# Nystrom attention and squared-ReLU MLP on one core: attention relaid by landmark segment, transposes moved from the DMA queue to TensorE and VectorE, instruction order written out as a table

## The chip, the core and the metric

One core of a Trainium2 chip. The time is device microseconds of one execution; 278.01 us is the median of three runs before the change (278.54, 278.01, 274.76).

## What is computed

For 8 batches of 8 heads, with q, k, v of 576 tokens by 64 (32 segments of 18 tokens each; a landmark is the mean of one segment):

```
q_lm, k_lm = segment means of q and k              # 32 x 64 a head
A  = softmax(q @ k_lm^T / 8)                       # 576 x 32
Bm = softmax(q_lm @ k_lm^T / 8)                    # 32 x 32
C  = softmax(q_lm @ k^T / 8)                       # 32 x 576
Z  = Bm^T / (norm1 * norminf);  6 times: Z = 2 Z - Z @ Bm @ Z
x  = A @ Z @ C @ v                                 # heads side by side: 4608 x 512
out = relu(x @ w_in)**2 @ w_out                    # 512 -> 2048 -> 512
```

## The kernel before

Batches follow each other. `attention(b)` makes, for one batch, AT (A transposed, heads on the partitions) and G (Z C v w_in, the product with `w_in` taken in early). `mlp_in(b)` forms h = G^T AT in 16 blocks of 128 hidden rows (L938, four matmuls of 288 columns a block), applies ReLU (L952, mostly ScalarE) and squares it into `gs` (L964 VectorE, L962 ScalarE). `mlp_out(b)` multiplies with `w_out` (L1004, 512 columns, 16 accumulated a tile), copies the tile out of PSUM (L375 ScalarE, L377 VectorE) and stores it (L978, SyncE's queue). Attention of batch b+1 is interleaved with the MLP of batch b.

Layout: a load (L441, GpSimd's queue, float32 in DRAM cast to bf16 on the way) puts six neighbouring tokens on each of 96 partitions. `kqraw` holds k and q of one batch and has one buffer; `vraw` has two. Landmark sums are matmuls with a 0/1 matrix (L547), and a second one folds and copies them (L560). K^T and Q^T come from TensorE transposes of 96 columns in batches 0 and 1 (L586) and from a DMA transpose in batches 2 to 7 (L529). The same split holds for C (L764, or the DMA transpose L775 into `ECT`) and for A (L901, or the DMA transpose L888 into `AT`). The scores of A are L843, of C L741, C v is L792, the iteration for Z is L696 (batch 0) and L701, its masked operand L640 on GpSimd, G is L916.

Order: every operation is registered with `add` and its dependencies. `Plan.emit` then simulates the engines with rough costs and places, again and again, the operation that can start first, with priorities and the offsets of the table `TUNE`. Each engine runs its own list in that order. In idle time of the first 36 us of the plan TensorE gets matmuls of zeros (L502).

Of the kernel before, what the change touches and what calls it, by code (L numbers as in the profile page):

```python
# [8 lines left out]
P = 128  # L9
AF = mybir.ActivationFunctionType  # L10
ALU = mybir.AluOpType
# [6 lines left out]
H = 8  # L18
# [7 lines left out]
TP = 96  # L26
NC6 = S // TP
NJ = NC6 // 2
HALF = S // 2
NG = 4  # L30
SCALE = 1.0 / 8.0
LN_EXP_SET = 6
LAG = 0.6
EARLY = 2
AHEAD = 0
Z = (0, 0, 0)
TUNE = [
    (75, 0, 0), (24, 0, 0), (24, 0, 0), (-179, 0, 0), (-175, 320, 0), (-225, 0, 0), (-152, 0, 0), (-100, 0, 0),
    (-168, 120, 0), (-63, 520, 0), (-152, 400, 0), (85, 160, 480), (-125, 0, 0), (-28, 0, 560), (-66, 0, 0),
    (93, 80, 0), (162, 120, 0), (-305, 320, 0), (50, 0, 0), (74, 0, 0), (339, 320, 0), (191, 480, 0),  # L40
    (277, 0, 640), (-96, 0, 0), (85, 40, 0), (-18, 0, 0), (15, 0, 0), (-229, 0, 0), (-292, 80, 0), (105, 120, 0),
    (-155, 0, 0), (-141, 0, 0), (-168, 40, 0), (33, 0, 0), (3, 280, 0), (124, 120, 0), (183, 0, 0),
    (134, 760, 0), (42, 0, 0), (55, 0, 0), (110, 80, 0), (-17, 0, 0), (327, 0, 0), (-40, 40, 0), (-87, 0, 0),
    (-76, 0, 0), (-80, 0, 80), (141, 120, 0), (-194, 0, 0), (-5, 280, 0), (-101, 200, 0), (11, 40, 0),
    (296, 400, 0), (-95, 0, 0), (324, 0, 0), (-168, 480, 0), (-209, 0, 0), (-250, 0, 400), (155, 520, 0),
    (-111, 0, 0), (-44, 40, -400), (-77, 0, 0), (-72, 0, 0), (391, 360, 0), (95, 0, 0), (340, 0, 400),
    (14, 0, 0), (42, 0, 0), (-125, 0, 0), (-27, 320, 0), (-258, 360, 0), (145, 0, 720), (35, 0, 0), (5, 200, 0),
    (15, 0, 0), (242, 0, 0), (76, 160, 160), (3, 0, 0), (-95, 80, 0), (21, 0, 0), (60, 0, 0), (-41, 0, 0),
    (12, 80, 0), (-141, 280, 0), (47, 0, 0), (-10, 0, 160), (-173, 0, 0), (-11, 0, 0), (-153, 360, 0),
    (166, 40, 0), (77, 0, 0), (-199, 0, 0), (-4, 0, 0), (-4, 40, 0), (108, 40, 0), (-115, 0, 0), (-106, 0, 0),  # L50
    (-46, 0, 0), (-151, 0, 0), (88, 0, 0), (56, 400, 0), (-88, 0, 0), (48, 0, 0), (225, 0, 0), (-87, 280, 0), Z,
    (1, 0, 0), (150, 160, 0), (13, 0, 0), (109, 120, 0), (-61, 800, 0), (59, 0, 0), (160, 800, 0), (154, 0, 0),
    (-194, 0, 0), (-10, 0, 0), (-307, 200, 0), (-84, 0, 0), (-140, 280, 0), (-102, 0, 0), (-253, 0, 0),
    (43, 0, 0), (-149, 560, 0), (66, 0, 0), (194, 40, 0), (-36, 80, -720), (-4, 0, -560), (29, 0, 0),
    (171, 160, 0), (54, 0, 0), (40, 0, 400), (29, 360, 80), (-232, 0, 0), (-146, 40, 0), (188, 40, 0),
    (-2, 0, 0), (-146, 200, 480), (159, 0, 720), (3, 0, 0), (132, 0, 480), (127, 120, 0), (-5, 0, 0),
    (-14, 80, 240), (-43, 0, 720), (29, 0, 0), (97, 760, -720), (86, 0, 0), (-94, 0, 0), (-144, 0, 0), (7, 0, 0),
    (-33, 360, -80), (42, 40, 0), (-254, 0, 0), (58, 0, 0), (106, 0, 0), (26, 0, 0), (-291, 0, 0), (-24, 0, 0),
    (165, 0, 0), (-162, 0, 0), (76, 0, 0), (-125, 80, 0), (383, 0, 0), (115, 80, 0), (31, 0, 0), (-211, 0, 0),
    (230, 280, 0), (45, 0, 0), (-19, 600, 0), (-153, 0, 0), (-129, 440, -320), (29, 0, 0), (-132, 360, 400),  # L60
    (243, 760, -400), (-163, 0, 0), (9, 0, 0), (-81, 40, 0), (39, 720, 0), (15, 0, 0), (-42, 280, 0),
    (-95, 0, -400), (-91, 40, 0), (195, 200, 0), (-107, 0, 0), (228, 40, 0), (-4, 320, 0), (74, 0, 0),
    (85, 0, 0), (-276, 0, 0), (-75, 600, 0), (-31, 0, 0), (46, 320, 0), (-222, 0, 0), (240, 0, 0), (-90, 0, 0),
    (50, 480, 0), (-136, 0, 0), (10, 280, 0), (-110, 280, 0), (75, 0, 0), (1, 0, 0), (-215, 0, 0), (-158, 0, 0),
    (104, 840, 0), (233, 0, 0), (-113, 0, 0), (63, 0, 0), (-147, 0, 0), (118, 0, -400), (-183, 0, 0),
    (-34, 320, 0), (255, 240, 0), (-75, 0, 0), (-198, 0, 0), (225, 0, 0), (-19, 760, 0), (-22, 40, 0),
    (62, 0, 0), (-372, 40, 0), (317, 0, 0), (265, 40, 720), (106, 400, 0), (-214, 0, 0), (119, 320, 320),
    (-73, 200, 240), Z, (-65, 560, 0), (-272, 200, -400), (-1, 0, 0), (-30, 0, -640), (-160, 240, 240),
    (-24, 0, 0), (-128, 80, -160), (-140, 0, -240), (43, 0, 0), (-118, 0, 80), (100, 840, 0), (225, 0, 0),
    (-124, 80, 0), (-1, 680, -800), (-183, 240, 0), (12, 0, 0), (25, 40, 0), (-97, 0, 0), (97, 80, 0),  # L70
    (-420, 760, -240), (167, 160, 0), (-11, 0, 0), (110, 360, 0), (117, 0, 0), (-25, 0, 0), (-1, 0, 0),
    (-64, 0, 0), (12, 0, 0), (-206, 0, 0), (356, 0, 0), (9, 0, 0), (-83, 0, 0), (-60, 0, 0), (26, 0, 0),
    (156, 0, 0), (189, 0, 0), (-93, 0, 0), (-57, 0, 0), (-101, 0, 720), (-169, 640, 0), (-89, 0, 0),
    (25, 160, 0), (-17, 0, 640), (-40, 0, 0), (33, 0, 240), (-146, 0, 160), (-65, 0, 0), (-242, 0, 0),
    (-344, 0, 0), (-66, 240, 0), (80, 0, 0), (54, 80, 0), (26, 0, 720), (-44, 0, 0), (-290, 120, 0), (-99, 0, 0),
    (104, 280, 0), (274, 120, 0), (8, 0, 0), (-117, 80, 0), (299, 0, 0), (141, 0, 0), (35, 0, 0), (103, 360, 0),
    (108, 0, 0), (-118, 0, 0), (-12, 200, 0), (140, 400, 0), (-254, 0, 0), (451, 200, 0), (187, 160, 0),
    (-69, 280, 0), (-18, 0, 0), (19, 120, 0), (248, 0, 0), (-104, 200, 0), (160, 0, 0), (-177, 0, 0), (96, 0, 0),
    (-186, 0, 0), (90, 160, 320), (27, 0, 0), (31, 0, 0), (-201, 600, 0), (129, 360, 0), (22, 0, 0),
    (-90, 40, 0), (-65, 120, 0), (-53, 0, 0), (-77, 0, 0), (94, 0, 0), (298, 0, 0), (103, 0, 560),  # L80
    (-130, 320, 0), (-181, 0, 0), (15, 0, 80), (-113, 120, 0), (41, 0, 0), (109, 0, 0), (215, 0, 560),
    (-164, 0, 0), (-195, 0, -720), (25, 0, 400), (-14, 0, 0), (-82, 120, -640), (249, 0, -80), (-20, 0, 0),
    (-17, 0, -240), (-312, 440, 0), (-10, 0, 0), (128, 240, -640), (145, 440, 480), (-74, 40, 0), (1, 0, 0),
    (11, 0, 0), (-168, 0, 0), (6, 0, 0), (-189, 640, 560), (-26, 200, 0), (21, 0, 0), (-76, 0, 0), (-12, 0, 0),
    (-1, 0, 0), (29, 0, 0), (66, 80, 0), (-121, 0, 0), (-5, 0, 0), (78, 80, 0), (-4, 0, 0), (91, 0, 0),
    (187, 0, 0), (-14, 0, 0), (46, 0, 0), (20, 0, 0), (60, 0, 0), (-127, 0, 0), (286, 440, 0), (-138, 400, 0),
    (18, 0, 0), (84, 600, 0), (152, 40, 0), (92, 0, 0), (65, 0, 0), (-111, 0, 0), (259, 600, -240), (-58, 80, 0),
    (52, 440, 0), (-31, 0, 0), (259, 440, 0), (-205, 0, 0), (84, 40, 0), (-188, 560, 0), (71, 0, 0),
    (-231, 0, 0), (-12, 0, 0), (-342, 0, 0), (158, 0, 0), (97, 0, 0), (-110, 0, 0), (149, 40, 0), (38, 0, 0),
    (54, 0, 0), (-151, 0, 0), (-239, 0, 0), (180, 0, 0), (-142, 320, 0), (87, 240, 0), (203, 0, 0), (405, 0, 0),  # L90
    (73, 0, 0), (19, 880, 0), (-38, 40, 0), (70, 480, -400), (131, 0, 0), (265, 320, 0), (103, 40, 0),
    (117, 0, 0), (19, 0, 0), (249, 240, 0), (-355, 40, 0), (318, 240, 0), (145, 40, 0), (193, 520, 0),
    (-144, 40, -400), (-367, 0, 480), (-76, 360, 0), (-111, 0, 0), (-163, 0, 0), (-241, 200, -240), (286, 0, 0),
    (-105, 0, -400), (70, 0, -160), (-69, 0, 0), (166, 0, 0), (-143, 160, 320), (22, 0, 0), (-177, 680, 0),
    (208, 240, 320), (4, 0, 0), (66, 240, 0), (207, 40, -560), (115, 0, 0), (-192, 880, 0), (-275, 0, -320),
    (-219, 0, 0), (-253, 0, 0), (122, 0, 0), (165, 0, 0), (-92, 40, 0), (98, 0, 0), (181, 680, 0), (75, 0, 0),
    (-59, 0, 0), (61, 0, 0), (-231, 0, 0), (217, 0, 0), (-213, 0, 0), (7, 160, 0), (-83, 40, 0), (30, 0, 0),
    (-144, 0, 0), (-75, 120, 0), (122, 0, 0), (-91, 0, 0), (-1, 40, 0), (-33, 0, 0), (-304, 200, 0),
    (155, 360, 0), (39, 0, -80), (-22, 560, 0), (89, 360, 0), (-25, 40, 0), (20, 120, -800), (-274, 0, 0),
    (125, 0, 720), (187, 0, -640), (215, 0, 0), (-235, 280, 0), (62, 480, 0), (13, 320, 0), (-261, 360, 0),  # L100
    (-67, 320, 0), (215, 520, 160), (-10, 40, 0), (-126, 0, 0), (-203, 440, 0), (3, 440, 0), (113, 0, 0),
# [976 lines left out]
```

## Time and profile before

| | |
|---|---|
| profiled execution: span | 274.2 us |
| runs: lowest, median, highest | 274.76, 278.01, 278.54 us |
| TensorE (PE) busy | 255.1 us, 93% |
| VectorE (DVE) busy | 188.1 us, 69% |
| ScalarE (ACT) busy | 168.6 us, 61% |
| GpSimd (POOL) busy | 98.1 us, 36% |
| q0, the loads of GpSimd's queue | 18.35 MB (bf16, as written), 44.3% of 16 DMA engines |
| q1, the stores and DMA transposes of SyncE's queue | 20.65 MB, 38.8% of 16 DMA engines |
| first matmul of the MLP (L938) | starts at 32.95 us |

The profiled execution has no time of its own beside the span; the span is 3.8 us below the median and 0.6 below the lowest run. In the profile's lines a group is "line engine operation out<-in", then the number of instructions; "busy us, mean ns" and the idle time ahead of them follow. A chain of waits is followed back from the last instruction, so its lines say what set the end. PEld is the loading of TensorE's weights, which runs beside the matmuls.

### The profile page before, as it was taken

What the parts mean: (1) busy time and instruction counts of PE and PEld (TensorE: products, weight loads), DVE (VectorE), ACT (ScalarE), POOL (GpSimd) and SP (SyncE); (2) the same over time, 40 slices, a digit from 0 to 9 for tenths busy, and PEclk for the clock granted to TensorE, in tenths of its full rate; (3) what the DMA queues carried; (4) which work ended last, traced back from release to release, by engine and by line L of the source; (5) the groups of instructions that cost most, each with busy time, mean ns of one, the idle gap of its engine ahead of it and who ended that gap; (6) DMA issues with size and microseconds to landing.
All of it is one profiled execution on the core that took longest, in us unless ns stands there. A gap on an engine that the chain in (4) does not pass through costs nothing.

```text
span 274.2 us, 7433 instructions
## 1 busy us (share of the span) xinstructions
PE 255.1 (93%) x2990; PEld 157.1 (57%) x3029; DVE 188.1 (69%) x440; ACT 168.6 (61%) x332; POOL 98.1 (36%) x143
## 2 busy tenths in 40 slices
PE   8868999997988999999989989999999999999993
PEld 8857767544654466546545556664644565555452
DVE  2497699887995689597857988799983557424200
ACT  1260789656984676688674678577870586658311
POOL 7544432643186116711843282272136103000000
PEclk9997999999999999999999999999999999999998
DMA  6999999699999999999999883299738110213122
GB/s 85 206 205 205 205 206 204 112 180 200 184 190 168 233 185 173 180 141 193 192 214 185 208 129 82 31 186 193 159 80 165 53 38 2 78 38 79 38 77 78
DMA packets 73346, 39.47 MB, mean 144 GB/s; under 512 B 46048, under 2 KB 68832, under 8 KB 73312
## 3 DMA queue, kind: packets, MB, share of 16 engines
q0 software_dynamic: 23040, 18.35, 44.3%
q1 hardware_dynamic: 50272, 20.65, 38.8%
q8 instruction: 23, 0.38, 0.5%
q14 instruction: 11, 0.09, 0.1%
HBM read 36.70 MB, written 9.44 MB: 168 GB/s over the span
## 4 chain that ended last, share of the span: by engine, by line
PE 55%; DMA 26%; DVE 7%; ACT 6%; issue 3%; POOL 2%; DVEq 0%; ACTq 0%; POOLq 0%
PE ps L1004 31%; DMA kqraw<-in_k_dram 15%; PE ps L938 15%; DMA ECT<-EC 4%; DMA kqT<-kqraw 4%; DVE gs L964 3%; ACT r L952 3%; DMA AT<-EA 2%; PE ps L916 2%; PE ps L547 2%; PE ps L843 1%; POOL EA L879 1%; PE ps L701 1%; DVE sA L868 1%; PE ps L792 1%
## 5 line engine op out<-in xcount | busy, mean ns | idle before, releaser
L1004 PE MATMUL ps<-w_out_bf,gs 128*128 128x512 bf16 (+1 forms) x553 | 139.1, 373 | 3.6 <-DVE gs L964 1.4
L952 ACT ACTIVATE r<-ps 128x576 bf16<-128x576 f32 x128 | 80.4, 648 | 26.0 <-PE ps L938 18.5
L1004 PEld LDWEIGHTS <-gs 128*128 128x128 bf16 x592 | 54.0, 98 | 48.4 <-issue 4.0
L938 PE MATMUL ps<-AT,G 128*128 128x288 bf16 x512 | 79.6, 286 | 1.1 <-DMA AT<-EA 0.3
L964 DVE TENSOR_TENSOR gs<-r 128x576 bf16<-128x576 bf16 x109 | 58.4, 555 | 17.7 <-ACT r L952 16.9
L938 PEld LDWEIGHTS <-G 128*128 128x128 bf16 x512 | 48.2, 98 | 24.2 <-issue 1.4
L640 POOL TENSOR_TENSOR Pd<-st,ones_d 128x256 bf16<-128x256 bf16 x42 | 30.1, 718 | 66.4 <-DVE st L712 57.1
L879 POOL TENSOR_TENSOR EA<-EA,rA 96x384 bf16<-96x384 bf16 x29 | 25.7, 902 | 9.6 <-DVE rA L872 6.5
L375 ACT CAST G<-ps 128x512 bf16<-128x512 f32 x40 | 21.7, 592 | 8.3 <-PE ps L916 8.0
L375 ACT COPY o<-ps 128x512 f32<-128x512 f32 (+1 forms) x23 | 13.0, 567 | 19.0 <-PE ps L1004 17.3
L852 DVE TENSOR_REDUCE mxA<-ps 96x16 f32<-96x512 f32 x24 | 16.1, 680 | 5.8 <-PE ps L843 5.7
L377 DVE CAST G<-ps 128x512 bf16<-128x512 f32 x24 | 15.9, 686 | 5.4 <-PE ps L916 4.7
L861 ACT ACTIVATE EA<-SA 96x512 bf16<-96x512 f32 x24 | 14.9, 627 | 7.6 <-DVE SA L855 7.2
L502 PE MATMUL ps<-zero 128*128 128x128 bf16 x181 | 15.9, 257 | 1.1 <-DVE zero L507 1.1
L712 DVE SCALAR_TENSOR_TENSOR st<-st,ps 128x128 bf16<-128x128 bf16 x40 | 11.1, 278 | 7.8 <-PE ps L701 5.7
L855 DVE TENSOR_TENSOR SA<-ps,mxA 96x512 f32<-96x512 f32 x24 | 16.2, 680 | 0.2
L377 DVE COPY o<-ps 128x512 f32<-128x512 f32 x14 | 9.7, 690 | 9.6 <-PE ps L1004 6.6
L752 ACT ACTIVATE EC<-ps,nmc 128x576 bf16<-128x576 f32 x16 | 11.8, 738 | 6.7 <-DVE nmc L747 5.2
L502 PEld LDWEIGHTS <-zero 128*128 128x128 bf16 x181 | 13.9, 118 | 1.9 <-DVE zero L507 1.1
L868 DVE TENSOR_REDUCE sA<-EA 96x24 f32<-96x768 bf16 x16 | 14.7, 937 | 0.2 <-ACT EA L861 0.2
L547 PEld LDWEIGHTS <-kqraw 96*128 96x128 bf16 x384 | 11.4, 96 | 3.0 <-DMA kqraw<-in_q_dram 1.3
L962 ACT ACTIVATE gs<-r 128x576 bf16<-128x576 bf16 x19 | 12.5, 683 | 0.5 <-PE ps L1004 0.2
(100 smaller groups left out, 240.5 us busy)
## 6 DMA issues: line engine op xcount, KB each, us to landing
kqraw<-in_k_dram POOLq DMA_DIRECT2D x8, 576.0 KB, 8.2
kqraw<-in_q_dram POOLq DMA_DIRECT2D x8, 576.0 KB, 11.3
vraw<-in_v_dram POOLq DMA_DIRECT2D x8, 576.0 KB, 11.6
out_dram<-o SPq DMA_DIRECT2D x23, 192.0 KB, 2.7
out_dram<-o SPq DMA_DIRECT2D x24, 128.0 KB, 2.6
w_in_bf<-in_moe_w_in_dram POOLq DMA_DIRECT2D x4, 512.0 KB, 11.2
w_out_bf<-in_moe_w_out_dram POOLq DMA_DIRECT2D x4, 512.0 KB, 21.1
out_dram<-o SPq DMA_DIRECT2D x23, 64.0 KB, 2.2
```

Source lines behind the costliest of these rows:

```text
L375: nc.scalar.copy(dst, src)
L377: ENG[e].tensor_copy(dst, src)
L502: mm(ps[:, bank, 0:P], lhsT=zero[:], rhs=zero[:], start=True, stop=True)
L547: mm(t[:, h, :], lhsT=raw[:, h, 2 * j:2 * j + 2, :].rearrange("p c d -> p (c d)"), rhs=seg[:], start=(j == 0), stop=(j == NJ - 1))
L640: ENG[e].tensor_tensor(dst[:], src.unsqueeze(2).to_broadcast([P, 2, NG, M]), ones_d[:].unsqueeze(1).to_broadcast([P, 2, NG, M]), ALU.mult)
L855: add({"DVE": dve(512)}, lambda e, sa=sa, j=j: nc.vector.tensor_tensor(grouped(SA[:, j, :]), grouped(one(sa)[0:TP, :]), mxA[:, j, :].unsqu ...
L868: add({"DVE": dve(768)}, lambda e, i=i: nc.vector.reduce_sum(sA[:, i, :, :].rearrange("p c g -> p (c g)"), EA[:, i, :, :].rearrange("p c ( ...
L879: ENG[e].tensor_tensor(w, w, rA[:, i, cs, :].rearrange("p c g -> p (c g)").unsqueeze(2) .to_broadcast([TP, NJ * NG, M]), ALU.mult)
L938: mm(t[:, j, 0:HALF], lhsT=G[:, i, f * P:(f + 1) * P], rhs=AT[:, i, j * HALF:(j + 1) * HALF], start=(i == 0), stop=(i == 1))
L952: nc.scalar.activation(rj, two(hk)[:, :, 0:HALF], AF.Relu)
L964: nc.vector.tensor_tensor(dst, r[:], r[:], ALU.mult)
L1004: mm(one(ok)[:, 0:hi - lo], lhsT=gs[:, f, x0:x0 + P], rhs=w_out_bf[:, f, lo:hi], start=(f == f0), stop=(f == f1 - 1))
```

## The change

1. A partition holds one landmark segment (18 tokens) of one head: 4 heads by 32 segments make 128 partitions, twice. k and q have two buffers each.
2. Landmark sums leave TensorE: five tree additions a half batch on VectorE or GpSimd (batch 0: VectorE reductions of the float32 data), then two TensorE transposes and one scaled copy.
3. K^T, Q^T and C are transposed on TensorE in every batch (36 and 9 transposes of 128 columns a batch), A with VectorE's 32x32 block transposes. No DMA transpose is left.
4. The score matmuls of A are 64x32 tiles with 32 columns, eight at a time on the array.
5. k and q of batch 0 come as float32 over SyncE's queue into the space of `gs`, in eight pieces, and are cast on ScalarE (seven) and GpSimd (one). All loads of GpSimd's queue wait for the last of the eight pieces (`hold`).
6. A stored tile is one transfer (two where it spans batches), its rows taken by segment.
7. `Plan.emit` follows `ORDER`, a list of 2019 codes for operation, engine and PSUM bank. In it 85 squares are on ScalarE (19 before) and 27 ReLUs on VectorE (none before).

The core of the diff:

```diff
-    kqraw = sb.tile([TP, 2, H, NC6, D], BF16, name="kqraw")
+    raws = {nm: [sb.tile([P, 2, SEG, D], BF16, name="%sraw%d" % (nm, i)) for i in range(2)] for nm in names}
...
-            nc.gpsimd.dma_start(dst, src[b].rearrange("h (p c) d -> p h c d", c=NC6))
+        return src[b].rearrange("(g i) (r t) d -> i g r (t d)", i=2, t=SEG)[i]
...
+                nc.sync.dma_start(stage[:, w, i, cut], rows(src, 0, i)[:, :, cut])
...
+    hold = add("hold", "POOL", lambda e: nc.gpsimd.tensor_copy(held[:], stage[:, 0, 1, NJ * D:NJ * D + 1]),
+               reads=[("k", "stage", 3)], writes=["held"])
+    load("v", 0, gate=[hold])
...
-                        mm(t[:, h, :], lhsT=raw[:, h, 2 * j:2 * j + 2, :].rearrange("p c d -> p (c d)"),
-                           rhs=seg[:], start=(j == 0), stop=(j == NJ - 1))
+                        ("add9", half[:, i, :, :], raw[:, i, 0:NJ, :], raw[:, i, NJ:SEG, :], [(nm, z, i)], "half"),
...
-                nc.sync.dma_start(kqTs[z][:, 0:2 * HT].rearrange("p (a t) -> p a t", t=TP),
-                                  kqraw.rearrange("p w h c d -> p (w h c d)"), transpose=True)
+                        nc.tensor.transpose(
+                            t[:, x * P:(x + 1) * P],
+                            raw[:, i, 2 * j:2 * j + 2, :].rearrange("p t d -> p (t d)"), ident[:])
...
-                    mm(t[:, :, x0:x0 + M], lhsT=kqTs[z][:, HT + y0:HT + y0 + P], rhs=kbd[:, h, :, :],
+                            mm(t[M * g:M * g + M, c, j * M:j * M + M],
+                               lhsT=Ts["q"][z][64 * c:64 * c + 64, NJ * i + j, g, :],
+                               rhs=dups["k"][64 * c:64 * c + 64, i, g, :], start=True, stop=True)
...
-                nc.sync.dma_start(AT.rearrange("p i (c t) -> p (i c) t", t=TP),
-                                  EA.rearrange("p i c x -> p (i c x)"), transpose=True)
+            add("a_xp", "DVE", lambda e, i=i: nc.vector.transpose(
+                AT[:, i, :], EA[:, i, :, :].rearrange("p t m -> p (t m)")),
...
-                    nc.sync.dma_start(rows[a:a + m, tok, lo:hi], osb[p0:p0 + m, lo:hi])
+            to = out[b * S:(b + 1) * S, :].rearrange("(r t) n -> t r n", t=SEG)
+                nc.sync.dma_start(to[t0:t1, :, lo:hi], osb[p0:p0 + n, lo:hi])
...
-    plan.emit()
+    plan.emit(ORDER)
```

## The prediction

> **What bounds it now.** The profile's first line first, then busy time by stretches of the execution.
>
> ```profile
> PE 255.1 (93%) x2990; PEld 157.1 (57%) x3029; DVE 188.1 (69%) x440; ACT 168.6 (61%) x332; POOL 98.1 (36%) x143
> ```
>
> ```profile
> 30.00:50.00 20.00, 19.07 (x311) 13.30 (x313) 18.52 (x45) 17.87 (x37) 6.45 (x10) 1.00 1.28 205
> 50.00:100.00 50.00, 45.98 (x503) 25.53 (x511) 40.51 (x94) 33.26 (x70) 21.66 (x29) 1.00 1.08 180
> 100.00:150.00 50.00, 47.58 (x562) 28.27 (x569) 38.54 (x91) 33.91 (x69) 23.47 (x32) 1.00 1.22 184
> 150.00:200.00 50.00, 48.58 (x563) 29.43 (x570) 43.58 (x98) 37.08 (x75) 19.19 (x26) 1.00 0.70 137
> 200.00:250.00 50.00, 49.63 (x449) 27.01 (x455) 25.80 (x56) 29.32 (x53) 10.67 (x15) 1.00 0.28 68
> ```
>
> Columns: stretch, length, busy us of PE, PEld, DVE, ACT, POOL, then granted clock, DMA share, GB/s. PE is the bound from 30 us on: it idles 0.93, 4.02, 2.42, 1.42 and 0.37 us in the five stretches. What ends the stalls is seen in the chain of waits in order of time (start, us, what); PE has other work beside most of each wait, so only the idle time above is lost:
>
> ```profile
> 52.58 10.45 DMA kqT<-kqraw
> 80.40 5.73 DMA ECT<-EC
> 103.16 5.18 DMA ECT<-EC
> 116.70 6.27 DMA AT<-EA
> ```
>
> Ahead of 30 us PE mostly waits or multiplies zeros. The timeline (start, us, instruction) gives the head: k usable, q usable, the first 32x32 product, Z finished, the first matmul of the MLP.
>
> ```profile
> 7.78 1.19 PE L586 MATMUL ps<-ident,kqraw 96*128 96x96 bf16 x24 [0.78 <-DMA kqraw<-in_k_dram]
> 10.63 0.77 PE L547 MATMUL ps<-seg,kqraw 96*128 96x32 bf16 x24
> 13.30 0.23 PE L608 MATMUL ps<-kdup,qpart 128*32 128x32 bf16 x8
> 26.23 0.20 DVE L727 SCALAR_TENSOR_TENSOR zt<-st,ps 128x64 bf16<-128x64 bf16 x1
> 32.95 0.30 PE L938 MATMUL ps<-AT,G 128*128 128x288 bf16 x1
> ```
>
> So the span has three parts: 33.0 us of head, 236.6 us in which PE is nearly full, and 4.6 us from the last matmul (269.6) to the end of the last store.
>
> **PE's own work.** Prices are the step from matmul to matmul inside a run: (length of the run - mean of one)/(number - 1).
>
> ```profile
> L586 PE MATMUL ps<-ident,kqraw 96*128 96x96 bf16 x96 | 4.9, 206 | 1.3 <-DMA kqraw<-in_k_dram 1.3
> L764 PE MATMUL ps<-ident,EC 128*96 128x128 bf16 x24 | 2.0, 219 | 1.4 <-DVE SA L855 1.4
> L843 PE MATMUL ps<-kbd,kqT 128*128 128x64 bf16 x192 | 8.7, 193 | 1.3 <-DMA kqT<-kqraw 1.3
> ```
>
> A 96-column transpose steps by 42 ns (24 in 1.19 us), a 128-column one by 56 (runs of six), a landmark matmul by 25 (24 in 0.77), a score matmul L843 by 29 (eight in 0.40), the 48 small L792 by 29 for each wave of four. Removed: 384 landmark matmuls 9.6 us, 16 folds at 110 ns 1.8, 96 transposes of K and Q 4.0, 24 of C 1.3, 24 of A 1.0, 192 scores 5.6, 96 waves of C v 2.8; together 26.1. Added: 288 + 32 + 72 transposes of 128 columns at 56 ns 22.0; scores of A as 1152 tiles of 64x32, eight at once, 144 waves at 29 ns 4.2; C v in 72 waves 2.1; together 28.3. Net +2.2 us. The eight-wide wave has no row of its own with 32 columns (L916 runs eight at once with 512). If only four run together, 4.2 and 2.1 double: +8.5. If the 392 transposes step like the 96-column ones: -3.3. I take +2.2, by the rows of equal column count.
>
> **The head.** The eight pieces of k and q are 2304 KB of float32. A load of 1152 KB took 2.9 us of transfer (q is usable 2.9 us after k), so 5.8 us; landing adds 2.0 (a 64 KB store takes 2.2 in all):
>
> ```profile
> out_dram<-o SPq DMA_DIRECT2D x23, 192.0 KB, 2.7
> out_dram<-o SPq DMA_DIRECT2D x23, 64.0 KB, 2.2
> ```
>
> From 1.4 us on all pieces are in at 9.2. By the stores' own slope (128 KB more cost 0.5 us) the transfer takes 9.0 and they are in at 12.4. Behind that two strands run. Compute: reduce 0.75, add, transpose, scaled copy, product, about 2.2 us, so the first product is at 11.4 rather than 13.3; then 13.1 us to Z as now, 24.5; then the last softmax sum, reciprocal, GpSimd's product (1.5 x 0.827 of L879) and VectorE's transpose (no row of this size; 64 elements take 0.245 and 576 elements of other operations 0.46 to 0.75, I take 0.75), 3.0 in all, 27.5. Data: `hold` lets GpSimd's queue go at 9.2. First data takes 3.5 us (6.4 from issue to landing of k less 2.9), then k of batch 1, four pieces of `w_in` and v, 3200 KB of bf16 at the 199 KB/us of q, 16.1: the last `w_in` at 28.8. Its G matmul stands ahead of the first L938 in PE's list, so L938 starts at 29.2: -3.8 us. Ends: -5.5 (compute decides) and -0.6 (the slower pieces). In GpSimd's list the product of A stands behind an issue of `w_out` that waits for v (23.6); that is ahead of its operands.
>
> **Waits on the DMA queue.** Without DMA transposes, and with two buffers for k and q, stretches 50:100 and 100:150 should fall to the idle time of 150:200 (2 x 1.42): -3.6. That stretch still has DMA transposes in it; at the level of 200:250, which has nearly none, all three would give -6.7. I take the middle, -5.1; the bad end is 0, if other waits take their place. SyncE's queue loses 18 transposes (5.9 us of issue each for kqT) and 33 of its 74 stores: no cost.
>
> **VectorE, ScalarE, GpSimd.** Steps in back-to-back runs: ReLU on ScalarE 0.55, square 0.59 on ScalarE and 0.38 on VectorE, PSUM copy of 512 0.48 and 0.61, of a 768-wide transpose tile 0.68 and 0.47. ScalarE: +66 squares 39, +15 wide copies 10, +8 other copies 4, 7 casts 4, -27 ReLUs -15, the rest -5: +37 us. VectorE: 27 ReLUs 18, 31 wide copies 14, 24 masks 7, 76 tree additions 17, 8 reductions 5, 16 block transposes 11, -66 squares -25, the rest -8: +39. Both stay below PE: about 24 us a batch against 30. So 0 in the sum, hidden under PE. The cover is thin between the first L938 of batch 0 and that of batch 1, where the table orders 34 us of PE, 31 of VectorE and 30 of ScalarE. GpSimd gets 20 more issues at 0.8 us and the small additions, and loses part of the masks: 110 us, hidden.
>
> **Sum.** -3.8 - 5.1 + 2.2 = -6.7, or 267.5 us for the profiled execution's 274.2. That execution is 3.8 us below the median, so I put 278.0 - 6.7 = 271.3.
>
> **Rivals.** Quarter of the engines (slower). The pieces of k and q have 128 rows on one side and 4 groups of 32 on the other; so have the new stores. Every transfer of before leads with equal counts on both sides (96 and 96, 128 and 128), so no row tells whether such a transfer spreads over all 16 engines. If it gets 4, always the same, the pieces take 4 x 5.8 = 23.2 us: k and q are in at 26.6 instead of 9.2, `hold` keeps every other load until then, L938 starts at 46.6, +13.7 instead of -3.8. The last 128 KB of stores cost 1.6 rather than 0.4 (64 KB more cost 0.2 on the last, smaller stores): +1.2. Sum 13.7 + 1.2 - 5.1 + 2.2 = +12.0: 290.0. It decides as soon as k and q land after 13 us. [...] Chance 0.29.
>
> In-order engines eat the gain. VectorE was 93% and ScalarE 89% busy in 30:50, and the stretch of that kind grows to 34 us of PE work. At the 81% of 50:100, VectorE's 31 us need 38.3, +4.5, and no wait is saved: -3.8 + 2.2 + 4.5 = +2.9: 280.9. For it: 76 us more work on these two. Against it: no PE wait of note in 30:50 (0.93 idle). Chance 0.18.
>
> **Chances and range.** The forecast has 0.53; its own range is 263 (-5.5 - 6.7 - 3.3 = -15.5) to 280 (bad ends of the head and the waits, or of the waves), most of it 265 to 277. About 2% is what a measurement of this kernel can tell from no change, since its three runs spread by 1.4%; below 272.4 is faster, above 283.6 slower. Forecast: 0.39 faster, 0.14 same. In-order: 0.14 same, 0.04 slower. Quarter: 0.02 same, 0.27 slower. The range goes from 264 to 293, to take in the quarter case.
>
> **What would show it.** Right: the last cast of k or q on ScalarE starts before 13 us, the first matmul of the MLP near 29, PE idle below 1.5 us in each 50 us from 50 on, score runs of 72 within 0.5 us. Quarter: low GB/s until 25 us, zeros on PE until then, stores of 256 KB landing after some 6 us rather than 3. In-order: PE idle for VectorE or ScalarE between 30 and 65 us. The forecast is wrong if the first L938 comes after 33 us or if the idle of PE does not fall.

## The result and the profile after

The changed kernel takes 357.24 us (median of four runs, 354.96 to 360.96) against 277.92 for the kernel before: 1.289 times as long (95% interval 1.277 to 1.301). The ratio leaves out the execution of 360.96 us, which was a slow one. The forecast was 271.3 and its range ended at 293; the direction, the size and the range were all wrong. The profiled execution has a span of 353.3 us. First its busy time, then the stretches (stretch, length, busy us of PE, PEld, DVE, ACT, POOL, granted clock, DMA share, GB/s):

```profile
PE 273.0 (77%) x3956; PEld 167.8 (47%) x3956; DVE 214.7 (61%) x521; ACT 233.1 (66%) x385; POOL 107.9 (31%) x170
```

```profile
30.00:50.00 20.00, 6.68 (x73) 5.41 (x73) 8.50 (x21) 8.26 (x14) 7.21 (x11) 0.50 0.72 127
50.00:100.00 50.00, 38.18 (x932) 25.35 (x930) 33.16 (x88) 35.48 (x59) 25.01 (x41) 0.81 0.90 125
100.00:150.00 50.00, 44.76 (x615) 26.93 (x613) 43.50 (x116) 46.38 (x77) 26.44 (x42) 1.00 0.65 118
150.00:200.00 50.00, 46.24 (x692) 26.64 (x680) 39.20 (x91) 39.94 (x67) 20.01 (x29) 1.00 0.37 72
200.00:250.00 50.00, 44.32 (x581) 26.53 (x574) 33.96 (x91) 41.03 (x69) 14.31 (x21) 0.97 0.36 74
```

PE, 19.07 us busy of 20 between 30 and 50 us before, is now busy for 6.68 there, and between 100 and 250 us it idles 3.8 to 5.7 us in each 50, where the forecast had less than 1.5. The timeline shows why the start is late (SyncE's issues of the first pieces, the casts of the last two, the first matmul of the MLP):

```profile
0.81 1.92 SPq L343 DMA_DIRECT2D gs<-in_k_dram  x3
2.77 15.96 SPq L343 DMA_DIRECT2D gs<-in_q_dram  x4
18.77 3.01 SPq L343 DMA_DIRECT2D gs<-in_k_dram  x1
39.84 0.67 ACT L261 CAST kraw<-gs 128x576 bf16<-128x576 f32 x1 [2.22 <-DMA gs<-in_k_dram]
40.41 0.67 ACT L261 CAST qraw<-gs 128x576 bf16<-128x576 f32 x1
68.66 1.05 PE L740 MATMUL ps<-AT,G 128*128 128x288 bf16 x5
```

The last pieces of k and q are cast at 40 us instead of before 13, and SyncE itself is held for 16 us by four issues. The costliest groups (busy us, mean ns of one, idle before them and its cause) show a second loss:

```profile
L740 PE MATMUL ps<-AT,G 128*128 128x288 bf16 x512 | 81.6, 288 | 12.0 <-ACT EC L608 11.6
L608 ACT ACTIVATE EC<-ps,nmc 128x576 bf16<-128x576 f32 x16 | 42.4, 2797 | 4.5 <-DVE nmc L605 4.5
```

The exponential of C has the same size as before, where one took 738 ns; now it takes 2797, and the first products of the MLP (L740) wait behind it for 11.6 us in all. A third loss stands at the end, in the waits of SyncE's queue (total, times, longest):

```profile
SPq L865 <- DMA out_dram<-o: 9.9, 1, 9.9
```

Cut at the first matmul of the MLP and at PE's last one, the spans compare so (us; the last column is the run all_mended, below):

| part | before | forecast | after | all mended |
|---|---|---|---|---|
| head | 33.0 | 29.2 | 68.7 | 38.1 |
| middle | 236.6 | 233.6 | 268.9 | 250.9 |
| tail | 4.7 | 4.7 | 15.7 | 7.9 |
| span | 274.2 | 267.5 | 353.3 | 296.9 |

So of the 79 us lost, 35.7 are in the head, 32.3 in the middle and 11.0 in the tail.

### The profile page after: what moved, and what is told of

Its sections match the earlier page's. It is cut to its first block, busy times and chain, and to the rows that moved or that the text cites. A ratio compares the mean times of both kernels' runs of the same rounds, so it can differ in the third digit from the quotient of the medians.

```text
span 353.3 us, 9375 instructions
## 1 busy us (share of the span) xinstructions
PE 273.0 (77%) x3956; PEld 167.8 (47%) x3956; DVE 214.7 (61%) x521; ACT 233.1 (66%) x385; POOL 107.9 (31%) x170
## 4 chain that ended last, share of the span: by engine, by line
PE 59%; ACT 12%; DVE 9%; DMA 6%; SPq 5%; issue 5%; DVEq 0%; ACTq 0%
PE ps L801 28%; PE ps L740 15%; ACT EC L608 10%; DMA gs<-in_k_dram 6%; SPq L343 5%; PE ps L465 3%; PE ps L721 3%; PE ps L683 3%; PE ps L620 2%; PE ps L635 1%; PE ps L391 1%; DVE nmc L605 1%; DVE gs L766 1%; ACT gs L764 1%; DVE sA L703 1%
## 5 line engine op out<-in xcount | busy, mean ns | idle before, releaser
L740 PE MATMUL ps<-AT,G 128*128 128x288 bf16 x512 | 81.6, 288 | 12.0 <-ACT EC L608 11.6
L756 ACT ACTIVATE r<-ps 128x576 bf16<-128x576 f32 x101 | 64.5, 651 | 21.1 <-PE ps L740 16.0
L740 PEld LDWEIGHTS <-G 128*128 128x128 bf16 x512 | 48.1, 98 | 34.7 <-issue 14.3
L764 ACT ACTIVATE gs<-r 128x576 bf16<-128x576 bf16 x85 | 57.3, 691 | 5.4 <-DVE r L758 4.6
L608 ACT ACTIVATE EC<-ps,nmc 128x576 bf16<-128x576 f32 x16 | 42.4, 2797 | 4.5 <-DVE nmc L605 4.5
L511 POOL TENSOR_TENSOR Pd<-st,ones_d 128x256 bf16<-128x256 bf16 x25 | 17.1, 683 | 49.6 <-DVE st L577 38.2
L758 DVE TENSOR_SCALAR r<-ps 128x576 bf16<-128x576 f32 x27 | 20.4, 755 | 19.5 <-PE ps L740 18.6
L465 PE MATMUL ps<-ident,qraw 128*128 128x128 bf16 x144 | 13.0, 230 | 19.7 <-ACT qraw L261 19.2
L707 POOL TENSOR_TENSOR EA<-EA,rA 128x576 bf16<-128x576 bf16 x12 | 14.2, 1180 | 34.7 <-DVE rA L705 17.6
L766 DVE TENSOR_TENSOR gs<-r 128x576 bf16<-128x576 bf16 x43 | 22.2, 523 | 1.3 <-ACT r L756 0.9
L465 PE MATMUL ps<-ident,kraw 128*128 128x128 bf16 x144 | 14.0, 242 | 8.9 <-ACT kraw L261 8.9
L465 PEld LDWEIGHTS <-qraw 128*128 128x128 bf16 x144 | 10.0, 102 | 22.7 <-ACT qraw L261 19.7
L577 DVE SCALAR_TENSOR_TENSOR st<-st,ps 128x128 bf16<-128x128 bf16 x40 | 11.2, 281 | 14.3 <-PE ps L567 8.4
L695 DVE TENSOR_REDUCE mxA<-ps 128x18 f32<-128x576 f32 x16 | 12.1, 755 | 8.7 <-PE ps L683 5.3
L465 PEld LDWEIGHTS <-kraw 128*128 128x128 bf16 x144 | 11.1, 109 | 11.1 <-ACT kraw L261 9.4
## 6 DMA issues: line engine op xcount, KB each, us to landing
kraw<-in_k_dram POOLq DMA_DIRECT2D x14, 288.0 KB, 10.5
qraw<-in_q_dram POOLq DMA_DIRECT2D x14, 288.0 KB, 10.5
w_out_bf<-in_moe_w_out_dram POOLq DMA_DIRECT2D x4, 512.0 KB, 13.1
```

What stands on the lines that cost most here:

```text
L465: nc.tensor.transpose(t[:, x * P:(x + 1) * P], raw[:, i, 2 * j:2 * j + 2, :].rearrange("p t d -> p (t d)"), ident[:])
L511: ENG[e].tensor_tensor(dst[:], src.unsqueeze(2).to_broadcast([P, 2, NG, M]), ones_d[:].unsqueeze(1).to_broadcast([P, 2, NG, M]), ALU.mult)
L608: add("c_exp", "ACT", lambda e, sc=sc, i=i: nc.scalar.activation(EC[:, i, :].rearrange("p (r j c) -> p c j r", j=NJ, c=2), two(sc)[:, :, 0 ...
L740: mm(t[:, j, 0:HALF], lhsT=G[:, i, f * P:(f + 1) * P], rhs=AT[:, i, j * HALF:(j + 1) * HALF], start=(i == 0), stop=(i == 1))
L756: nc.scalar.activation(r.rearrange("p (j t) -> p j t", j=2), src, AF.Relu)
L758: nc.vector.tensor_scalar(out=r.rearrange("p (j t) -> p j t", j=2), in0=src, scalar1=0.0, scalar2=None, op0=ALU.max)
```

## The experiments

**Only the first loads in 32 rows.**

```
-  nc.sync.dma_start(stage[:, w, i, cut], rows(src, 0, i)[:, :, cut])
+  for g in range(NG):
+      nc.sync.dma_start(stage[M*g:M*g+M, w, i, cut], rows(src, 0, i)[g][:, cut])
```

> Only the first loads of k and q change: four transfers of 32 rows each for every piece. Quarter theory (4 engines carry a piece): pieces in before 15 us, first matmul of the MLP near 35 instead of 68.7, and the clock at 1.0 from there, so 357 - 35 = 322 us. Rival (GpSimd's loads, released at 7 us, crowd the engines and are themselves narrow): pieces still late, first matmul of the MLP after 55, 345 us or more.

Measured: 348.73 us, 1.255 times before (1.238 to 1.271). The last cast starts at 26.7 us and the first matmul of the MLP at 56.6. The rival was right: wide first pieces alone save 12 us of the head, because `hold` lets GpSimd's loads go at 4.4 us, and those are still narrow. The addresses are those of the change, and the first piece is cast at 4.3 us where it was 7.1: the shape of the transfer counts, not which rows it reads.

**Heads in order: 128 rows lead on both sides.**

```
-  src[b].rearrange("(g i) (r t) d -> i g r (t d)", i=2, t=SEG)[i]
+  src[b].rearrange("(i g) (r t) d -> i (g r) (t d)", i=2, t=SEG)[i]
   (v and the rows of w_in numbered alike; w_in in eight loads of 64 rows, not four of 128)
```

> Heads are numbered (i g) instead of (g i), so that 128 rows lead on both sides of all loads of k and q, first and later ones. Quarter theory: as the 32-row pieces or better, 318 us; if later loads mattered too, 310. If the head's half clock is its own cause (it does not come back with the early data), the first matmul of the MLP still comes after 45 us and the time stays above 330.

Measured: 324.74 us, 1.168 times before (1.156 to 1.181). The last cast starts at 12.6 us, the first matmul of the MLP at 38.1: 30.5 us of the head are the width of the loads, and GpSimd's loads had 18.5 of them. Middle (270.6) and tail (15.6) stay, and the mean granted clock from 20 to 40 us is still 0.56 to 0.59.

**The narrow pieces alone on the DMA engines.** GpSimd's loads wait for the last piece of q, and the last piece of k is issued fourth.

```
-  copy(held, stage[:, 0, 1, NJ*D:NJ*D+1])   # k, piece 3
+  copy(held, stage[:, 1, 1, NJ*D:NJ*D+1])   # q, piece 3
```

> The change as it is, but GpSimd's loads wait for the last piece of q, and the last piece of k goes fourth: the narrow pieces have the DMA engines to themselves. If 4 engines alone make them late, they take 4 x 5.8 = 23 us: last cast at 25 to 27 instead of 40, first matmul of the MLP near 58 (GpSimd's own narrow loads follow). If they are late because GpSimd's loads crowd them: last cast before 16, first matmul near 45.

Measured (353.27 us, one run; timeline: casts of pieces, and `hold`):

```profile
6.80 0.67 ACT L261 CAST kraw<-gs 128x576 bf16<-128x576 f32 x1 [4.71 <-DMA gs<-in_k_dram]
9.69 0.67 ACT L261 CAST kraw<-gs 128x576 bf16<-128x576 f32 x1 [2.22 <-DMA gs<-in_k_dram]
12.61 0.67 ACT L261 CAST kraw<-gs 128x576 bf16<-128x576 f32 x1 [2.25 <-DMA gs<-in_k_dram]
27.18 0.19 POOL L404 COPY held<-gs 128x1 f32<-128x1 f32 x1 [24.89 <-DMA gs<-in_q_dram]
```

A piece of 288 KB comes every 2.9 us, the time that 1152 KB took before: a quarter of the rate, and all are in at 27.2, where the rival "quarter of the engines" had 26.6. The rate is 101 GB/s (288 KB in 2.9 us); in the changed kernel, from 5 to 7 us, with these pieces alone under way, the DMA share is 0.26 at 100 GB/s, and in heads_in_order, whose pieces are wide, 0.81 at 251 GB/s over the first 10 us. The first matmul of the MLP is at 64.4, since GpSimd's narrow loads then follow. So the late data need no crowding to be late; the crowding adds the 12 us or so from here to the 39.8 of the changed kernel.

**The exponential of C written contiguously.**

```
-  EC[:, i, :].rearrange("p (r j c) -> p c j r", j=NJ, c=2)
+  EC[:, i, :].rearrange("p (j c r) -> p c j r", j=NJ, c=2)
```

> The exponential of C is written with 32 neighbouring elements together; the columns of C then stand in another token order than v's rows, nothing else changes. Stride theory: one exponential takes 0.75 us instead of 2.80, 16 x 2.05 = 33 us of ScalarE; PE waits 11.6 us for it directly, and ReLUs behind it are late too: 357 - 25 = 332. Rival (ScalarE is simply loaded, other waits take over): -12 at most, 345.

Measured: 342.13 us, 1.231 times before (1.216 to 1.246). One exponential takes 740 ns, and the middle shrinks from 268.9 to 253.1 us: 15.8, between the two theories. Half of ScalarE's 33 us had been hidden. The head stays at 68.8, so the exponential has no part in what was lost there.

**The exponential in four orders, two batches each.**

```
-  EC[:, i, :].rearrange("p (r j c) -> p c j r")   # read as "p c j r"
+  batches 0-1: "p (r j c) -> p c r j"             # read as "p c r j"
+  batches 2-3: "p (c r j) -> p c j r";  4-5: "p (j r c) -> p c j r"
```

> Heads in order; the exponential of C is written in four orders: batches 0-1 as the change (36-byte layout) but walked so that neighbours go 4 bytes apart, 2-3 with steps of 18 bytes, 4-5 of 4 bytes, 6-7 of 36 bytes as the change; 2 to 5 leave C's columns in another token order. If the step between neighbouring writes sets the price: 0.75 us in batches 0-1 and 4-5, about 2.8 in 2-3 and 6-7. If the layout does, however it is walked: 2.8 in 0-1. If it grows with the step: about 1.6 at 18 bytes.

Measured (317.18 us, one run; timeline: one of each pair of batches):

```profile
46.50 0.91 ACT L612 ACTIVATE EC<-ps,nmc 128x576 bf16<-128x576 f32 x1
100.48 2.81 ACT L612 ACTIVATE EC<-ps,nmc 128x576 bf16<-128x576 f32 x1
142.63 0.91 ACT L612 ACTIVATE EC<-ps,nmc 128x576 bf16<-128x576 f32 x1 [0.17 <-DVE nmc L609]
206.32 2.72 ACT L612 ACTIVATE EC<-ps,nmc 128x576 bf16<-128x576 f32 x1 [1.59 <-DVE nmc L609]
```

The step between neighbouring writes sets the price, not the layout: 0.91 us at 4 bytes, 2.81 at 18, 2.72 at 36. The first line has the change's own layout, walked with `j` innermost instead of `r`: swapping two letters on both sides of the instruction gives back 1.9 of the 2.06 us.

**Heads in order, exponential contiguous, stores in 32 rows.**

```
-  nc.tensor.transpose(t[:, x*P:(x+1)*P], raw[:, i, 2*j:2*j+2, :], ident[:])   # k
+  for c in range(2):
+      nc.tensor.transpose(t[64*c:64*c+64, x*P:(x+1)*P], raw[:, i, NJ*c+j, :], ident[:])
-  nc.sync.dma_start(to[t0:t1, :, lo:hi], osb[p0:p0+n, lo:hi])
+  for x in range(t1 - t0):
+      nc.sync.dma_start(to[t0+x, :, lo:hi], osb[p0+M*x:p0+M*x+M, lo:hi])
   (EC written as (j i c r), v's rows ordered alike; heads as above)
```

> Heads in order, the exponential of C contiguous (K transposed in 64-column halves so that v's rows match, +18 PE transposes a batch), stores in 32-row transfers. If narrow transfers and the stride are the whole loss: 357 - 38 - 25 - 3 + 5 = 296 or less, near the forecast's 271 if the rest of its sum holds. If VectorE and ScalarE, loaded with 76 us more, hold PE up (the in-order rival), 290 to 300 with PE idle 3 us or more in each 50.

Measured: 300.56 us, 1.081 times before (1.073 to 1.088): head 40.3, middle 251.1, tail 8.9. The 32-row stores take 6.8 us off the tail; what is left of it is SyncE's 0.42 us for each of the many issues.

**Half of the small score products.**

```
-  for c in range(2):      # 72 products of 64x32 tiles
+  for c in range(1):      # 36, and 4 of 288 columns for the rest
```

> As the version with all three mends; of each 72 score products of A (64x32 tiles) the 36 of the upper rows are replaced by 4 of 288 columns (wrong order, same amount), so 40 instead of 72. If each small matmul costs its own 9.2 ns however many run at once: a run falls from 0.66 us to 0.33 + 0.1 = 0.43, PE -3.7 us in all. If a wave costs 73 ns whatever its width, as the forecast's waves: 9 waves still 0.66, + 0.1.

Measured: 295.44 us (one run; the base has 300.56). PE's timeline, first this run, then the version it is based on:

```profile
22.19 0.42 PE L702 MATMUL ps<-kdup,qT 64*32 64x32 bf16 x36
```

```profile
23.42 0.72 PE L702 MATMUL ps<-kdup,qT 64*32 64x32 bf16 x72
24.88 0.66 PE L702 MATMUL ps<-kdup,qT 64*32 64x32 bf16 x64
29.39 0.23 PE L702 MATMUL ps<-kdup,qT 64*32 64x32 bf16 x8 [3.86 <-issue]
```

Where no wait follows, the 504 small products from the first matmul of the MLP on step by 8.6 ns with four tiles side by side, the 1008 of the base by 8.3 with eight: each costs its own step here, and a wave gains nothing from being wider. These products take 6.3 us instead of 8.3, the wide ones included, a gain of 2.0 where 3.7 were expected. The stall of 3.86 us in the middle of a run, in which PE waited for nothing that the profile shows, is down to 0.7, and the first matmul of the MLP comes at 34.7 instead of 40.3.

**Loads held to the last piece.** The edit of narrow_alone on the version heads_exp_stores.

> As the version with all three mends; the last piece of k is issued fourth instead of last, and GpSimd's loads wait for the last piece of q instead of the third of k. If the loads released at 3.9 us steal the engines from the first pieces: all pieces in at 9.5 instead of 12.4, first matmul of the MLP at 36 to 37 instead of 40.3, time 297. If the weights then are what is late: w_in moves from 23 to 29, first matmul at 40 or later, no gain.

Measured: 299.58 us (one run), span 297.6, first matmul of the MLP at 38.2, `hold` released at 10.2 and not 9.5. A gain of 2.1 us in the head, between the two expectations.

**All mended.** Heads in order, exponential walked with `j` innermost, loads held, stores in 32 rows, in the tail on SyncE's and ScalarE's queues in turn; K transposed as in the change.

```
-  nc.sync.dma_start(to[t0+x, ...], ...)
+  (nc.scalar if tail and x % 2 else nc.sync).dma_start(to[t0+x, ...], ...)
```

> Heads in order; the exponential of C walked so that neighbours go 4 bytes apart, in the change's layout; loads held to the last piece of q; stores in 32 rows, in the tail on two queues. Sum against the 297.6 us of hold_to_last_piece: no split of K, 126 transposes at 30 ns, -3.8; tail -3; exponentials 0.17 us longer, off the path: 291. What then stays above before's 274 is PE's small matmuls (+9), the head, and the rest of the waits. If GpSimd's or VectorE's load were what holds PE, it would not fall below 296.

Measured: 298.74 us, 1.079 times before (1.066 to 1.092). Against hold_to_last_piece the tail gained 1.1 us and the middle nothing: without the split of K PE's busy time falls by 1.8 us and its idle time grows by 2.3. PE's longest waits after the head are of two kinds (total, times, longest):

```profile
PE ps L654 <- DVE Zd L583: 2.5, 3, 1.8
PE ps L804 <- issue: 2.3, 1, 2.3
PE ps L684 <- issue: 2.0, 2, 1.3
```

2.5 us wait for Z, 4.3 for nothing shown. The run stayed above 296, where the expectation put the load of VectorE or GpSimd as the cause. VectorE ends 4.5 us of PE's waits here and 1.6 in before, but PE's idle time as a whole, 9.5 us, is about that of before (9.3), so this load is not what keeps the run above; the gain that failed to come is the one foreseen from the split of K. None of the mends brings the change to the level of the kernel before.

## Why the prediction was wrong, step by step

**The head, -3.8: wrong, +35.7.** The failing step is the transfer of the eight pieces, put at 5.8 us on 16 engines. They run at a quarter of that rate, as narrow_alone shows on idle engines (2.9 us for 288 KB, before for 1152). The share of 0.26 in the changed kernel (5 to 7 us) amounts to 4.2 of 16 engines. The prediction held this up as a rival at 0.29; no row of before showed its 4, and this share and narrow_alone's 2.9 us are what the runs show for it. With 32 or 128 leading rows on both sides (first_by_32, heads_in_order) the first piece is cast at 4.3 and 3.8 us and not at 7.1; how other shapes spread over the engines, no run shows. The rival was also priced too low (46.6 for the first matmul of the MLP, 68.7 measured): it made only the first pieces narrow, while GpSimd's 28 loads of k and q have the same shape (10.5 us from issue to landing, 5.1 and 6.8 in all_mended), and it let `hold` wait for all pieces, as the list of changes has it too. `hold` reads one, the first that is issued, so GpSimd's loads start at 7.3 us and share the engines with the rest.

Even with wide loads the head is 38.1 and not 29.2. In hold_to_last_piece the pieces are in at 10.2, near the forecast's 9.2, but the first 32x32 product comes 7.0 us later instead of 2.2: a reduction takes 1.14 us and not 0.75, and VectorE has eight of them. From the product to Z pass 15.2 us instead of 13.1, with a PE stall of 3.7 in them; scores_half_small, with a stall of 0.7, starts the MLP at 34.7.

**The exponential, inside "the rest -5" of ScalarE: wrong.** It was counted at its old price because its shape had not changed. Its output pattern had: neighbours now go 36 bytes apart. That is +33 us of ScalarE, 15.8 us of time. One exponential takes 0.74 us with neighbours 2 bytes apart, 0.91 at 4 bytes, 2.81 at 18 and 2.72 at 36; where between 4 and 18 bytes the price jumps, and by what mechanism, no run shows.

**PE's own work, +2.2: mis-sized.** A step is the time from the start of one matmul to the start of the next; ahead of a gap, which may hide a wait or a missing record, it is taken as the median of its kind. Without the two large products, PE's steps from the first matmul of the MLP on add up to 35.1 us before and 48.0 after, +12.9 (about 1 us of this is work on batch 1 that the kernel before does ahead of that matmul). The terms most out are the waves: 29 ns was taken for eight tiles, 72 were measured (1008 products in 9.1 us, 3.7 forecast; a run of 72 takes 0.72 us or more, not 0.5), and 72 for C v (504 in 4.5, 1.8 forecast). The row that would have told it was there: L792's 48 small products run at 7 ns each, four to a wave. Reading that as "a wave" instead of "four products" was the error, and the bad end named for it, 58 ns, was still too low. The 128-column transposes (56) were sized right: 58 ns.

**The waits on the DMA queue, -5.1: half of it was not there.** The idle time in before's stretches was taken for waits on transfers. What ended PE's waits there (total, times, longest; of the waits of 0.3 us and less, only those for transfers):

```profile
PE ps L1004 <- DVE gs L964: 1.4, 2, 0.8
PE ps L843 <- DMA kqT<-kqraw: 1.3, 1, 1.3
PE ps L701 <- POOL Pd L640: 1.0, 2, 0.7
PE ps L792 <- DMA ECT<-EC: 0.8, 2, 0.5
PE ps L1004 <- issue: 0.6, 4, 0.2
PE ps L938 <- DMA AT<-EA: 0.3, 1, 0.3
PE ps L547 <- DMA kqraw<-in_k_dram: 0.2, 1, 0.2
```

Of the 9.3 us in which PE idles behind the head, transfers ended 2.6, other engines some 3.4. The remaining 3.3 are short gaps and "issue", and most of these gaps stand where a record is missing, as the two groups of the output product show:

```profile
L1004 PE MATMUL ps<-w_out_bf,gs 128*128 128x512 bf16 (+1 forms) x553 | 139.1, 373 | 3.6 <-DVE gs L964 1.4
L1004 PEld LDWEIGHTS <-gs 128*128 128x128 bf16 x592 | 54.0, 98 | 48.4 <-issue 4.0
```

592 weight loads and 553 matmuls: 39 are not recorded. A missing one leaves a gap of only some 50 to 65 ns (twice 216 ns from start to start, less the 373 that a record lasts), so all of them make 2 to 3 us and not more. The chain's transfers of 5 us and more cost PE some 2.6 us together, and hardly more was to be had by taking them out. Even that did not show: all_mended, without any DMA transpose, idles 9.5 us behind its head, on other waits.

**VectorE, ScalarE and GpSimd at 0: right but for the exponential.** In all_mended ScalarE is busy 37.8 us longer than before (forecast 37), VectorE 26.3 (39), GpSimd 105.9 in all (110), and PE waits for VectorE 4.5 us in the whole middle (0.7, 0.6, 0.4 and 0.3 beside the 2.5 shown). The in-order rival's condition did not come about; in the changed kernel ScalarE did hold PE, but by the slow exponential. (In that rival's sum 38.3 less 34 is 4.3, not 4.5; nothing hangs on it.)

**The tail, 0: wrong, +11.0.** The quarter rival had +1.2, for the last 128 KB alone. But five tiles, 1.3 MB, are stored from 333 us on, and from 335 to 350 the DMA share is 0.21 to 0.27 at 69 to 99 GB/s, the rate of narrow_alone at best. So the last store, in pieces of 1 KB, is waited for 9.9 us behind the others.

**What closes and what stays open.** Loads 30.5, exponential 15.8, stores 6.8 and PE's small work 12.9 make 66 of the 79 us. all_mended still is 22.6 us above before: head 5.1 (a stall of 2.9 in it), tail 3.2, middle 14.3. Of the middle 12.3 are PE's small work (47.4 against 35.1); PE's idle time there, 9.5 us against 9.3, is no part of it. The mends took 56.4 us back, some 3 more than loads, exponential and stores give one by one; how much of this is the second queue, the held loads and the waits that went with them was not told apart.

## What to carry to other kernels

Before pricing a new layout, write down for every transfer the leading size on both sides, and for every write the distance between neighbours: two rearrange patterns cost 46 us here and were mended by renumbering the heads and by swapping two loop letters. Price a run of small matmuls per instruction (8.3 and 8.6 ns each here, with eight and with four side by side), not per wave. Before counting PE's idle time as waits to be won, list what ended each wait, and compare the numbers of matmuls and of weight loads: of 9.3 us here, the DMA queue had 2.6.

## What was not expected of the hardware

- A slow issue held its queue: four issues of narrow loads kept SyncE 16 us in the changed kernel, and a store's issue in the tail took 2.8 us, against 0.3 to 0.6 in the tail of before.
- The activation that writes 36 bytes apart also made its accumulator read longer, 490 ns in the changed kernel against 196 before.
- In all ten runs of the new layout PE stops in the head behind its 351st matmul, waiting for nothing that the profile shows: 0.7 us in scores_half_small, 3.7 and 3.9 in hold_to_last_piece and heads_exp_stores, 4.4 in the changed kernel, 6.0 in exp_contiguous. Which instruction that is differs: the 64th product of a run in two of them, the sixth of eight of L562 in the changed kernel. So the gap goes with a place in PE's list and not with one operand. In seven of the ten a 16 KB transfer of the instruction queue starts inside the gap (in the changed kernel at 55.8 us, the gap is 55.5 to 59.9), in narrow_alone 0.4 us ahead of it. That the instructions came late is the author's reading; no run tried it by itself.
- The granted clock was 0.5 from 7.5 to 68.9 us in the changed kernel. In exp_contiguous and narrow_alone the view prints 1.0 for most of the head, but the traces have no clock record there before 47.7 and 65.0 us. Six transposes (L465) take 0.82 us in these stretches, as at 0.5 in the changed kernel, and 0.50 at 1.0: a stretch without records is not one at full clock. What the half clock costs in the head was not measured.
